# Banded heads as query columns of two 64-key blocks with packed sinks, and where q and k are transposed and evacuated (one core, attention plus expert layers)

## The chip, the cores and the metric

One core of one Trainium2 chip. The metric is device time in microseconds; lower is better. A run is called slow when it took over 1.5% longer than the fastest run of the same kernel, and fast otherwise; only fast runs enter a ratio, but the medians given are over all runs. The runs fell on several chips. Kernels are compared only within the same rounds.

Engines: TensorE (PE), VectorE (DVE), ScalarE (ACT), GpSimd (POOL). PSUM is the memory that the matmuls write into; to evacuate is to copy a result out of it. The clock is the share of TensorE's full clock that was granted, by the trace's record of its changes (the clock record). Times in a trace count from the start of the profiled run.

## The reference

```python
# attention: 4 batches, 8 heads, 768 tokens, head size 64; heads 0, 2, 6 are full, the others banded
keep_full   = i >= j
keep_banded = (i >= j) & ((j < 4) | (i - j < 64))      # 4 sink keys and a window of 64
a = softmax(where(keep, q @ k.T / 8, -1e9)); x = a @ v # x: 3072 tokens x 512
# expert layers: every token goes to the expert of its domain_id (8 experts)
out[t] = relu(x[t] @ w1[e]) @ w2[e]
```

## The kernel before

The heads are worked in 16 pairs, four per batch: (0,2) two full heads (RR), (6,7) one full and one banded (RS), (1,3) and (4,5) two banded (SS). For a pair, TensorE puts a mask into PSUM as a matmul with the identity, adds the scores, ScalarE takes the exponential, and the values are multiplied one pair later. In between TensorE transposes q and k of the next pair. Twenty routing items (token counts, ranks, one-hot rows, the map from slots to tokens) are threaded in, mostly on VectorE; two of them, `ranks` and `rows`, have matmuls that wait for VectorE.

PSUM: three wide tiles (1024 fp32) for scores, and two small banks for transposes, values and the routing matmuls.

```python
def tr(t, ...):                      # q and k each in a small bank, in different steps
    ...
        evac = nc.scalar.copy if n == 0 and nm == "q" else nc.vector.tensor_copy
        evac(out=d[:], in_=cell["ps"][:, 0:NSO].rearrange("d t p -> d p t"))
# ... cut
for n in range(NPAIR + 1):
    hooks(n)                         # loads, casts on GpSimd, stores
    R = len(plans[n % 4])            # score tiles: RR 6, RS 5, SS 3
    if R == 3:
        steps = [T["q"] + A, T["k"] + B_]              # A, B_: values of the pair before, head by head
    else:
        steps = [T["q"] + A, T["k"] + B_[:h], B_[h:]]
    for x, step in enumerate(steps):
        scores(n, range(2 * x, min(2 * x + 2, R)))
        if n >= 1 and route:
            route.pop(0)()           # one routing item after each group of scores
        run(step)
```

The softmax here doesn't subtract the row's maximum and nothing guards it: scores larger than these inputs give would overflow.

## Time and profile before

Median 215.31 us in three runs (212.85 to 215.68). The profile is of a slow run (227.59 us); a profile on another chip (225.17 us) has its attention part within 2 us of it. Read from the two traces by the q transposition in each pair, which is one easily found row per pair:

| | before | before, other chip |
|---|---|---|
| first scores of pair 0 | 8.52 | 8.52 |
| q transposition for pair 10 | 59.14 | 58.41 |
| q transposition for pair 15 | 83.46 | 81.97 |
| first expert-layer matmul | 97.80 | 94.52 |

The timeline of TensorE at the start of pair 1 (columns: start, duration, engine, line, operation, result and operands, sizes, count, and in brackets the idle time before it with what ended it):

```profile
14.78 0.62 PE L306 MATMUL sp<-qT,kT 64*128 64x512 f16 x9
15.33 0.51 PE L286 MATMUL tpq<-c16s,q 128*128 128x128 f16 x6
...
17.36 0.30 PE L484 MATMUL prior_ps<-rs,c16s 128*128 128x8 f16 x3
17.74 0.49 PE L286 MATMUL tpk<-c16s,k 128*128 128x128 f16 x6
```

The rank matmuls (prior_ps) stand between two groups without any wait, and six transposes take 0.5 us.

### The profile page before, as it was taken

How to read it: one execution, taken by the hardware profiler on the slowest of the kernel's cores; microseconds unless marked ns; L12 is line 12 of the kernel's file. 1: busy time of each engine (PE TensorE's matmuls, PEld its weight loads, DVE VectorE, ACT ScalarE, POOL GpSimd, SP SyncE). 2: the span in 40 equal slices, each digit the busy share in tenths (PEclk: the TensorE clock that was granted, in tenths of full speed). 3: DMA queues.
4: the chain of work that ended last, by engine and by line, in shares of the span. 5: the costliest groups of instructions: out<-in, count | busy, mean ns of one | idle time of the engine just before them, and what ended most of it. 6: DMA issues, size and time to landing. Idle time of an engine off the chain costs nothing. (4 is left out here: it accounts for less than half of the span.)

```text
span 225.8 us, 4791 instructions
## 1 busy us (share of the span) xinstructions
PE 187.7 (83%) x1959; PEld 123.0 (54%) x1959; DVE 98.7 (44%) x200; ACT 92.1 (41%) x120; POOL 120.7 (53%) x170
## 2 busy tenths in 40 slices
PE   0888779989899999289969499999999999998430
PEld 0455455656576675169958495455554564443210
DVE  1448999998977574142110105520244002433210
ACT  2487248855775885115634260025400461000000
POOL 2446768774666884740178743657566403027611
PEclk9999999999999999859997999999999999999955
DMA  6999999999999998399649999996999999704321
GB/s 190 325 298 312 288 299 298 328 291 281 280 343 320 216 249 172 107 170 235 167 90 212 207 256 209 256 219 185 183 185 280 214 220 279 201 17 168 131 93 48
DMA packets 42909, 49.79 MB, mean 220 GB/s; under 512 B 27263, under 2 KB 35712, under 8 KB 42882
## 3 DMA queue, kind: packets, MB, share of 16 engines
q0 software_dynamic: 7936, 26.75, 52.9%
q1 hardware_dynamic: 34802, 22.62, 35.2%
q8 instruction: 17, 0.28, 0.5%
q10 hardware_dynamic: 144, 0.07, 0.2%
q14 instruction: 10, 0.08, 0.1%
HBM read 56.76 MB, written 10.49 MB: 298 GB/s over the span
## 5 line engine op out<-in xcount | busy, mean ns | idle before, releaser
L343 ACT ACTIVATE eT<-sp 128x1024 f16<-128x1024 f32 (+2 forms) x68 | 57.4, 919 | 28.5 <-PE sp L306 26.0
L718 ACT ACTIVATE hT<-h 128x512 f16<-128x512 f32 (+2 forms) x48 | 32.1, 668 | 62.5 <-PE h L711 61.3
L711 PE MATMUL h<-xT,w 128*128 128x256 f16 (+2 forms) x384 | 53.6, 302 | 0.4 <-issue 0.4
L727 POOL DMA_INDIRECT out_dram<-oute,out_i x27 | 27.0, 1001 | 38.7 <-DVE oute L725 33.0
L711 PEld LDWEIGHTS <-w 128*128 128x128 f16 x384 | 40.6, 117 | 11.5 <-issue 0.6
L761 PE MATMUL o<-w,hT 128*128 128x512 f16 x184 | 41.9, 379 | 0.0
L725 DVE COPY oute<-o 128x512 f32<-128x512 f32 x23 | 15.9, 691 | 55.2 <-PE o L761 47.6
L663 POOL DMA_INDIRECT xe<-x_tok,map_i x24 | 24.4, 1019 | 23.7 <-SPq L932 13.1
L396 PE MATMUL av<-ve,eT 128*128 128x65 f16 (+1 forms) x472 | 24.6, 196 | 5.5 <-remote 3.0
L761 PEld LDWEIGHTS <-hT 128*128 128x128 f16 x184 | 17.5, 98 | 19.8 <-issue 0.8
L396 PEld LDWEIGHTS <-eT 128*128 128x128 f16 (+1 forms) x572 | 21.6, 101 | 10.9 <-DVE xb L409 3.9
L306 PE MATMUL sp<-qT,kT 64*128 64x192 f16 (+8 forms) x276 | 23.6, 273 | 2.8 <-DVE kT L292 2.6
L306 PE MATMUL sp<-c16s 128*128 128x128 f16 (+1 forms) x132 | 21.6, 271 | 1.9 <-ACT eT L343 1.7
L158 POOL CAST q<-q 128x768 f16<-128x768 f32 x15 | 12.4, 829 | 15.0 <-DMA q<-in_q_dram 6.4
L178 POOL CAST ve<-v 128x384 f16<-128x384 f32 x32 | 17.0, 558 | 5.5 <-DMA v<-in_v_dram 5.5
L696 DVE COPY xT<-xtp 128x1024 f16<-128x1024 f16 (+1 forms) x16 | 8.8, 552 | 24.0 <-PE xtp L683 24.0
L409 DVE TENSOR_TENSOR xb<-av,rcp 128x384 f16<-128x384 f32 x32 | 17.8, 557 | 1.1
L292 DVE COPY qT<-tpq 128x768 f16<-128x768 f16 x15 | 14.3, 953 | 8.9 <-PE tpq L286 8.9
L158 POOL CAST k<-k 128x768 f16<-128x768 f32 x15 | 13.6, 904 | 7.9 <-PE tpk L286 4.3
L306 PEld LDWEIGHTS <-kT 64*128 64x128 f16 (+1 forms) x276 | 10.8, 96 | 12.4 <-DVE kT L292 4.3
L292 DVE COPY kT<-tpk 128x768 f16<-128x768 f16 x16 | 15.2, 953 | 3.7 <-PE tpk L286 3.7
L753 ACT COPY oute_last<-o_last 128x128 f32<-128x128 f32 x2 | 0.5, 265 | 32.2 <-DVE oute_last L753 32.2
(83 smaller groups left out, 148.4 us busy)
## 6 DMA issues: line engine op xcount, KB each, us to landing
w<-in_moe_w_dram POOLq DMA_DIRECT2D x16, 1024.0 KB
q<-in_q_dram SPq DMA_DIRECT2D x16, 384.0 KB, 5.9
k<-in_k_dram SPq DMA_DIRECT2D x16, 384.0 KB, 6.0
v<-in_v_dram SPq DMA_DIRECT2D x32, 192.0 KB, 5.8
x_tok<-xb SPq DMA_DIRECT2D x4, 768.0 KB, 7.9
out_dram<-oute,out_i POOLq DMA_INDIRECT x27
xe<-x_tok,map_i POOLq DMA_INDIRECT x24
c16s<-c SPq DMA_DIRECT2D x1, 336.5 KB, 5.5
```

Of the source, the lines that this page charges most:

```text
L158: eng.tensor_copy(out=t[:].rearrange("p t h d -> p h t d"), in_=q32_t[nm, n][:])
L178: nc.gpsimd.tensor_copy(out=ve_t[b][:, :, h, 0:D], in_=v_t[b, pi][:, hh])
L292: evac(out=d[:], in_=cell["ps"][:, 0:NSO].rearrange("d t p -> d p t"))
L306: nc.tensor.matmul(out=sp[rows, c : c + w], lhsT=lhsT, rhs=rhs, start=bank not in begun, stop=True, skip_group_check=True,)
L343: nc.scalar.activation(out=eT[n, r // 3][:, r % 3, c0:c1], in_=sp[:, c0:c1], func=AF.Exp, scale=scale)
L396: nc.tensor.matmul(out=ps[m0:m1, it, :], lhsT=eT[n, r // 3][:, r % 3, c : c + w], rhs=rhs, start=(x == 0), stop=(x == len(mms) - 1), skip_ ...
L409: nc.vector.tensor_tensor(out=xb[b][:, :, h * D : (h + 1) * D], in0=ps[:, :, 0:D], in1=rcp[:].unsqueeze(2).to_broadcast([P, NSO, D]), op=A ...
L663: nc.gpsimd.indirect_dma_start(out=xe_of(pr, g), out_offset=None, in_=x_d[0 : 1 + nb * S, :], in_offset=bass.IndirectOffsetOnAxis(ap=map_i ...
L711: nc.tensor.matmul(out=pv[:, a, c0:c1], lhsT=w_t[e, 1][:, c // 2, c % 2, fc * 512 + fr : (fc + 1) * 512 : 4], rhs=xT_t[e][:, c, c0:c1], st ...
L718: nc.scalar.activation(out=hT_t[e][:, 2 * f2 : 2 * f2 + 2, c0:c1], in_=pv[:, :, c0:c1], func=AF.Relu)
L727: inst = nc.gpsimd.indirect_dma_start(out=out, out_offset=bass.IndirectOffsetOnAxis(ap=out_i[:, s : s + 1], axis=0), in_=o[:], in_offset=None,
L761: nc.tensor.matmul(out=ps[:], lhsT=hT_t[e][:, f, g * P : (g + 1) * P], rhs=w_t[e, 2][:, f // 4, f % 4, :], start=(f == 0), stop=(f == 7),)
```

## The change

Its intent: a banded head's scores are laid out so that each query column meets only the two 64-key blocks that its window can reach, which removes one of three score tiles; the sinks of several heads are packed into one stationary tile of v; q and k are transposed in one go, in a wide tile for SS pairs (with q evacuated by ScalarE) and in both small banks otherwise; the value matmuls of the half blocks need a shifted copy of v (vm), made by VectorE. Its core:

```diff
+    def copy_vm(n):                                     # two copies per pair with a banded head
+        for rows, t0 in ((slice(0, 64), 1), (slice(64, P), 0)):
+            nc.vector.tensor_copy(out=vm_t[b][rows, ...], in_=ve_t[b][rows, t0 : t0 + NSO - 1, ...])
...
+    def transposes(n, q_evac, wide):
+        if wide:
+            ps = ps_s.tile([P, 2, 8, P], FP16, tag="sp", ...)      # q and k in one wide tile
+        else:                                                      # q and k in the two small banks
+            halves = [ps_b.tile([P, 8, P], FP16, tag="b", ...)[:] for nm in "qk"]
+        ... 12 transposes ...
+        for x, (nm, store, evac) in enumerate((("q", qT, q_evac), ("k", kT, nc.vector.tensor_copy))):
+            evac(out=d[:], in_=halves[x][:, 0:NSO].rearrange("d t p -> d p t"))
...
-            if n >= 1 and route:
-                route.pop(0)()
-            run(step)
+            run(step)
+            if n >= 1 and R > 1 and (R, x) != (3, 1):   # R counts steps now: RR 3, RS 2, SS 1
+                for fn in route[:2]:
+                    fn()
+                del route[:2]
```

```diff
-        if R == 3: steps = [T["q"] + A, T["k"] + B_]
-        else:      steps = [T["q"] + A, T["k"] + B_[:h], B_[h:]]
+        steps = {1: [tr + av0 + av1 + post],            # post: copy_vm(n)
+                 2: [tr + post, av0 + av1],
+                 3: [tr, av0, av1]}[R]
```

Not shown: the new masks and score bins, the value matmuls in 64-row halves, six zero-filled sink tiles at the start with six small loads.

## The prediction

> **What bounds the kernel now.** I read the page first (state, busy shares, slices), then engine windows cut at the first scores of each batch, then the timeline of single pairs, then the waits. The profiled execution is a slow one (227.59 us against a median of 215.31), so I use it for durations and order inside the attention part, where the clock was granted in full, and not for the end-to-end time.
>
> ```profile
> span 225.8 us, 4791 instructions
> PE 187.7 (83%) x1959; PEld 123.0 (54%) x1959; DVE 98.7 (44%) x200; ACT 92.1 (41%) x120; POOL 120.7 (53%) x170
> ...
> PE   0888779989899999289969499999999999998430
> ...
> DVE  1448999998977574142110105520244002433210
> ACT  2487248855775885115634260025400461000000
> ```
>
> The slices (5.6 us each) split the run: about 16 slices of attention, where VectorE is at 8 to 9 in slices 4 to 10 and falls afterwards, a hole at slice 17, then the expert layers, which the change does not touch. The windows say the same in numbers (columns: engine busy us and count, clock, DMA share, GB/s). The four batches of four head pairs are the first four lines; the last two are pairs 1 to 9 and pairs 10 to 15.
>
> ```profile
> 14.78:32.33 17.55, 13.66 (x225) 9.52 (x224) 15.53 (x37) 9.34 (x11) 12.14 (x23) 1.00 1.16 296
> 32.33:52.24 19.91, 18.48 (x293) 12.41 (x294) 19.60 (x39) 14.31 (x17) 16.15 (x25) 1.00 1.09 299
> 52.24:72.48 20.24, 19.11 (x317) 12.99 (x318) 16.10 (x38) 14.42 (x17) 11.21 (x23) 1.00 1.12 311
> 72.48:90.04 17.56, 17.01 (x279) 11.43 (x277) 10.46 (x20) 13.54 (x16) 12.54 (x21) 1.00 1.00 222
> 14.78:64.19 49.41, 43.13 (x694) 29.09 (x693) 45.32 (x101) 32.88 (x39) 34.67 (x60) 1.00 1.12 298
> 64.19:90.04 25.85, 25.13 (x419) 17.26 (x418) 16.36 (x31) 18.74 (x22) 17.38 (x31) 1.00 1.05 256
> ```
>
> Two regimes. In pairs 1 to 9 VectorE is busy 45.3 of 49.4 us (19.60 of 19.91 in the second batch), because the token routing (49 instructions, 21 us, added up from the timeline) is threaded between the evacuations. In pairs 10 to 15 TensorE is busy 25.13 of 25.85 us and VectorE has room. ScalarE binds only in the pair of two full heads: six exponentials, some 5.5 us. One stretch of VectorE's timeline shows how a transpose evacuation, a division and a routing step follow each other without a gap:
>
> ```profile
> 43.68 0.68 DVE L584 TENSOR_TENSOR ohl<-c16s,lof 128x512 f16<-128x512 f16 x1
> 44.28 0.95 DVE L292 COPY qT<-tpq 128x768 f16<-128x768 f16 x1
> 45.15 0.18 DVE L408 RECIPROCAL rcp<-av 128x6 f32<-128x6 f32 x1
> 45.36 0.56 DVE L409 TENSOR_TENSOR xb<-av,rcp 128x384 f16<-128x384 f32 x1
> 45.84 1.07 DVE L584 TENSOR_TENSOR ohl<-c16s,lof 128x512 f16<-128x512 f16 x1
> ```
>
> The DMA queues move about 300 GB/s throughout (share above 1), but TensorE waits for GpSimd's casts only 1 us in all, so loads are near a limit and not yet the limit.
>
> **What the Trainium skill says.** "TensorE: Matmul & The Clock Gate", section "Wait — 56ns, not 53.3ns?": a warm matmul costs N/2.4 GHz plus 2.5 ns, and starts never come closer than about 25 ns. The trace agrees: six transposes take 0.51 us from first start to last end, one lasts 0.22, so (0.51 - 0.22)/5 = 58 ns; 21 value matmuls of 65 columns take 0.80 us, one 0.195, so 30 ns. "TensorEngine Tiling (Array Packing)", section "Tiling Modes": 64x64 gives four independent tiles, and a mode switch drains the array; column tiling disables the fast weight load. Nothing in this trace shows four tiles at once; 64-column weight loads do read longer (111 ns against 98). "VectorE: DVE Perf Modes", section "The perf-mode tier table": a 16-bit copy inside SBUF can go at 4x, one out of PSUM at most at 2x. The PSUM side agrees (768 elements in 953 ns, below even 2x with that strided output); no plain fp16 SBUF copy is in the trace, the nearest is a 672-element multiply in 417 ns. "TensorE: Matmul & The Clock Gate", section "Why this matters for your kernels": an idle gap over about 3 us cools the clock. Here the granted clock fell to 0.64 and 0.50 between 94 and 100 us after such a hole.
>
> **The change part by part.** Write RR for two full heads, RS for one full and one banded, SS for two banded; a batch has one RR, one RS, two SS.
>
> ScalarE. SS drops its third score tile: 8 exponentials of 704 columns, 6.1 us. RS drops from 4x1024+256 to 3x1024+640 columns, about 0.7 us each by 1.02 us per 1024, 2.8 us. It takes over seven q evacuations (the one ScalarE did measured 0.80): +5.6 us. Net -3 us on an engine that is busy 75% at most: worth little directly.
>
> TensorE, SS pair. From the timeline of pair 11 (67.69 to 72.15 us): masks 0.97, 12 score matmuls 0.55, q transposes 0.35, values 0.68, small masks 0.16, 6 more scores 0.50, k transposes 0.56, values 0.69: 4.46 us. After: mask columns 2176 to 1536, so 0.97 x 1536/2048 = 0.73; 34 small score matmuls at 30 ns, 1.02, plus about 0.1 for drains; 12 transposes 0.70; 32 value matmuls, as many as before, 1.3. Sum 3.85: 0.6 less. This assumes the tiles really overlap; without overlap the scores alone would be near 1.9 us and the gain gone. RS: masks somewhat fewer, seven matmuls net more: TensorE about equal at 4.3 us, but five ScalarE tiles become four (4.5 to 3.8 us); pair 13 ran 4.99 us, so perhaps 0.4 to be had. RR unchanged. The whole order has 140 more weight-load and matmul pairs.
>
> VectorE. Removed: seven q evacuations of 0.953, 6.7 us. Added: 24 half-height copies of v, 8 of 330 and 16 of 660 elements; from the 417 ns row I estimate 0.24 and 0.40 us, 8.3 us. Six zero fills of 512 words at the start: the 256-word one took 272 ns, so 0.53 each and about 4 us with the small ones, from 1.1 us until just when q lands (4.87): 0 to 0.3 us of delay. In pairs 1 to 9 alone: -4 x 0.953 + 6 x 0.24 + 8 x 0.40 = +0.8, so about 46 us of VectorE work in a stretch of 49.4. The change does not relieve the engine that binds there. It also bunches the routing: four steps in each RR and RS pair, none in SS, so RR plus RS of the second batch carry about 16 us of VectorE work against 10 us of the others', and SS about 3 us against 4. The first batch could gain 1 to 2 us (its VectorE was idle 2 us), the third can lose as much: the map matmuls stand on TensorE between two score steps and wait for the last one-hot step.
>
> GpSimd. 20 sink copies (5.2 us) and four fills leave, six load issues come (0.78 us each by the weight loads' rows). Even; not on the path.
>
> The sum. Pairs 1 to 9: -1 us, give or take 2. Pairs 10 and 11: -1.2. Pairs 12 to 15: TensorE -1.6, but hidden in part: the third batch's token store was issued at 77.83, its first gather began at 87.31 and the first gathered transpose at 91.48, while TensorE was through with pair 14's values at 90.04. That chain of 13.7 us does not shorten, so I count a third of it, 0.5. Total about -2.7 us: 215.3 - 2.7 = 212.6.
>
> **The rivals.** (a) VectorE stays the bound in the routing part and the bunching costs more than the slack: the second batch's 98.5% speaks for it, the hole in the first batch against. Pairs 1 to 9 would be 2 us longer and the whole even: 215. (b) The small tiles do not overlap, or each drain costs: SS keeps its 4.46 us; 214 to 216. Longer 64-column weight loads speak for it; the alternating 64-row matmuls (12 in 0.62 us) against. (c) Everything fits: SS at 3.85 us, the copies at their fastest, ScalarE's earlier q evacuations keep TensorE fed, and the store lands sooner in an undisturbed run than in this slow one: 8 x 0.6 + 4 x 0.4 + 1.5 = 8 us, 207. That so many placements were chosen by hand speaks for it. (d) The wait for the gathers grows past 3 us and cools the clock: plus 1 to 3 us.
>
> **Range and chances.** I predict 212.6 us. The range 208.0 to 217.0 holds (a), (b) and most of (c). Faster by over 2% means below 211.0, which needs most of (c): 0.34. Slower by over 2% (above 219.6) needs (a), (b) and (d) together: 0.07. Within 2%: 0.59.
>
> **What would show it.** In the changed profile: an SS pair without routing takes about 3.9 us from scores to scores; VectorE above 90% busy over pairs 1 to 9, which take 47 to 50 us; value copies of 0.24 and 0.40 us; the routed RR and RS pairs each over 6 us; TensorE waiting longer than before ahead of the gathered transposes; expert layers unchanged. Wrong if SS pairs stay at 4.4 us (tiles do not overlap), if pairs 1 to 9 fall well below 47 us (then the evacuations' order, not VectorE's sum, had set the pace), or if the time moves in the expert layers.

## The result, and the profile after

232.75 us median in four runs (229.62 to 233.26), against 215.5 us for the kernel before in the same call. The ratio of the fast runs is 1.0796, 95% interval 1.0612 to 1.0981. (A ratio is the mean time of one kernel's fast runs over that of the other's of the same rounds, so it is not quite the ratio of the medians.) The change is slower. Run again on another chip (below, with the experiments), it was 1.0833.

The profiled run (233.26 us) counts as slow, 1.6% above the fastest. The repeat was profiled in a fast run, and its pairs 1, 4, 9 and 13 (12.95, 6.77, 10.92 and 5.45 us) bear out what is read here.

The page of the changed kernel; the second line is TensorE's busy share in tenths per slice, the third the granted clock in tenths, which answers to the page shown in the prediction:

```profile
span 231.5 us, 5105 instructions
...
PE   0675985997775985994995789999999999999960
...
PEclk9985599599999599998599999999999999999996
```

The clock has fives inside the attention part (slices 4, 5, 8, 14, counted from 1). In the kernel before it had none there. Windows of single pairs, cut at their first scores (pairs 1, 4, 9 and 14), and the whole of pairs 1 to 9; the clock is the third number from the end:

```profile
16.19:28.97 12.78, 9.95 (x91) 6.06 (x91) 5.38 (x14) 3.66 (x4) 6.01 (x10) 0.50 1.13 282
38.90:46.48 7.58, 6.97 (x73) 4.02 (x74) 6.62 (x21) 5.17 (x6) 2.56 (x4) 0.57 1.07 296
68.17:79.50 11.33, 8.84 (x112) 5.73 (x113) 7.50 (x19) 3.66 (x4) 2.50 (x4) 0.76 1.04 308
100.43:104.75 4.32, 3.50 (x88) 2.63 (x88) 1.50 (x3) 2.63 (x3) 0.00 (x0) 1.00 0.73 229
16.19:79.50 63.31, 49.50 (x771) 32.58 (x772) 46.70 (x107) 31.86 (x36) 29.51 (x48) 0.80 1.05 277
```

Pairs 1 to 9 took 63.31 us where the kernel before took 49.41 (its window is in the prediction). VectorE is busy 46.70 us of them, almost what it was (45.32): it was not given much more to do, it was waited for. The pair lengths, scores to scores:

| pair | kind | before | after |
|---|---|---|---|
| 1 | RS | 5.21 | 12.78 |
| 2 | SS | 6.85 | 4.49 |
| 4 | RR | 5.60 | 7.58 |
| 9 | RS | 5.60 | 11.33 |
| 12 | RR | 5.60 | 6.61 |
| 13 | RS | 4.84 | 5.45 |

Values of pair 14 were done at 107.25 us, not 90.04, and the first expert-layer matmul came at 112.38 instead of 97.80. From there to the end of the span it took 119.1 us in this trace and 119.0 in the repeat. All of the loss is in the attention part.

The waits of the changed kernel (who waited for whom, us in total, times, longest):

```profile
DVE kT L315 <- ACT qT L315: 10.7, 6, 2.8
...
PE sp L342 <- DVE kT L315: 6.9, 8, 1.5
...
PE av L392 <- DVE vm L186: 3.0, 3, 2.3
PE prior_ps L484 <- DVE rs L473: 2.8, 1, 2.8
```

And TensorE's timeline in pair 1, to be laid beside the rows of the kernel before:

```profile
15.90 0.36 PE L325 MATMUL sp<-c16s 128*128 128x128 f16 x2 [0.48 <-ACT eT L353]
16.19 2.58 PE L342 MATMUL sp<-qT,kT 64*128 64x512 f16 x20
18.70 0.82 PE L306 MATMUL tpq<-c16s,q 128*128 128x128 f16 x6
...
22.99 0.31 PE L484 MATMUL prior_ps<-rs,c16s 128*128 128x8 f16 x3 [2.83 <-DVE rs L473]
...
25.27 2.49 PE L392 MATMUL av<-ve,eT 128*128 128x65 f16 x42
```

Two things are to be seen. TensorE stood still for 2.83 us in front of the rank matmuls. And everything around them runs at half speed, already before that halt: six transposes take 0.82 us, not 0.51; the 20 score matmuls take 2.58 us, while the same 20 take 1.69 in pair 13; the 42 value matmuls take 2.49, in pair 5 1.44. Adding up these differences over pair 1 gives 4.15 us (0.89 scores, 0.65 transposes, 0.22 masks, 0.68 scores, 1.05 values, 0.66 masks). 2.83 + 4.15 = 6.98 of the 7.57 us that pair 1 is longer. In pair 9 the halts are 0.71 and 1.77 us (ahead of the map matmuls), the slow matmuls behind them 0.68 + 1.05 + 0.66 = 2.39: 4.9 of 5.7 us.

```profile
71.34 0.68 PE L595 MATMUL map_ps<-ohh,ohl 128*128 128x56 f16 x20 [0.71 <-DVE qT L315]
73.80 0.28 PE L595 MATMUL map_ps<-ohh,ohl 128*128 128x56 f16 x4 [1.77 <-DVE ohl L584]
```

Why pair 1 is slow from its first matmul is seen in pair 0. The same 3.41 us of it, in the kernel before and in the changed one (windows; TensorE's busy time is the second number after the window, the clock the third from the end):

```profile
12.65:16.06 3.41, 2.74 (x40) 1.72 (x39) 1.69 (x4) 2.82 (x4) 1.43 (x2) 1.00 1.19 300
12.65:16.06 3.41, 1.98 (x18) 0.81 (x14) 0.73 (x1) 3.06 (x4) 1.69 (x3) 1.00 1.29 265
```

The kernel before stopped for 0.19 and 0.48 us in it and ran on at full clock; the changed kernel stopped for 0.68, 0.26 and 0.48 us, waiting for exponentials, and its clock fell at 16.06.

Pairs 2 to 4 show two more things, in one stretch of the timelines of ScalarE, VectorE and TensorE:

```profile
31.61 0.81 ACT L315 COPY qT<-tp 128x768 f16<-128x768 f16 x1
32.45 0.96 DVE L315 COPY kT<-tp 128x768 f16<-128x768 f16 x1 [1.84 <-ACT qT L315]
33.46 0.87 PE L342 MATMUL sp<-qT,kT 64*128 64x128 f16 x34 [0.72 <-DVE kT L315]
34.71 3.13 DVE L186 COPY vm<-ve 64x660 f16<-64x660 f16 x2
37.90 0.19 PE L392 MATMUL av<-vm,eT 128*64 128x65 f16 x1 [2.28 <-DVE vm L186]
```

In the banded pairs k is evacuated only when ScalarE is through with q, which itself stands behind two exponentials: VectorE idles 1.84 us, then TensorE 0.72. And two copies of v took 3.13 us, though the median of all 24 is 0.38 us and the shortest 0.24; GpSimd was casting during all of it. TensorE waited 2.28 us, and pair 4 then ran at a clock of 0.57.

From this come four theories. A: the routing, bunched behind the steps, halts TensorE at `ranks` and `rows`. B: the order q before k in the shared tile delays every banded pair. C: the small score tiles and their interleaving cost TensorE itself. D: the v copies on VectorE are slow beside GpSimd and delay what stands behind them. Over all of them stands the clock: is the half speed a cause of its own, set off by any of these halts, or only a companion?

### The profile page after: what moved, and what is told of

It reads as the page before. It is cut to its first block, busy times and chain, and to the rows that moved or that the text cites. A ratio compares the mean times of both kernels' runs of the same rounds, so it can differ in the third digit from the quotient of the medians.

```text
span 231.5 us, 5105 instructions
## 1 busy us (share of the span) xinstructions
PE 188.0 (81%) x2099; PEld 123.2 (53%) x2099; DVE 104.3 (45%) x229; ACT 90.3 (39%) x115; POOL 116.6 (50%) x152
## 5 line engine op out<-in xcount | busy, mean ns | idle before, releaser
L353 ACT ACTIVATE eT<-sp 128x1024 f16<-128x1024 f32 (+2 forms) x56 | 50.7, 953 | 43.1 <-PE sp L342 42.8
L711 PE MATMUL h<-xT,w 128*128 128x256 f16 (+2 forms) x384 | 51.7, 295 | 0.4 <-DVE xT L690 0.4
L711 PEld LDWEIGHTS <-w 128*128 128x128 f16 x384 | 39.3, 115 | 11.2 <-DVE xT L690 0.6
L725 DVE COPY oute<-o 128x512 f32<-128x512 f32 x23 | 15.9, 692 | 51.7 <-PE o L761 49.5
L342 PE MATMUL sp<-qT,kT 64*64 64x128 f16 (+6 forms) x436 | 28.2, 272 | 6.9 <-DVE kT L315 6.9
L761 PEld LDWEIGHTS <-hT 128*128 128x128 f16 x184 | 17.5, 98 | 19.8 <-issue 0.8
L392 PE MATMUL av<-ve,eT 128*128 128x65 f16 (+1 forms) x372 | 21.1, 209 | 3.5 <-DVE qT L315 1.5
L342 PEld LDWEIGHTS <-kT 64*64 64x64 f16 (+2 forms) x436 | 12.6, 109 | 19.6 <-DVE kT L315 8.7
L325 PE MATMUL sp<-c16s 128*128 128x128 f16 (+2 forms) x112 | 18.9, 294 | 1.9 <-ACT eT L353 1.9
L186 DVE COPY vm<-ve 64x660 f16<-64x660 f16 (+1 forms) x24 | 13.9, 577 | 0.2
L683 PE MATMUL xtp<-c16s,xe 128*128 128x128 f16 x96 | 8.6, 227 | 5.4 <-DMA xe<-x_tok,map_i 5.4
L315 DVE COPY qT<-tpq 128x768 f16<-128x768 f16 x8 | 7.7, 958 | 11.4 <-PE tpq L306 11.3
```

The costliest lines, as they stand in the source:

```text
L325: nc.tensor.matmul(out=sp[:, c : c + w], lhsT=id_sb, rhs=c16[:, col : col + w], start=c // 512 not in begun, stop=True, skip_group_check=True,
L342: nc.tensor.matmul(out=sp[o : o + m, c : c + w], lhsT=kT[n][rows, k0 : k0 + m], rhs=qT[n][rows, i0 : i0 + w], start=False, stop=True, skip ...
L353: nc.scalar.activation(out=eT[n, r // 3][:, r % 3, c0:c1], in_=sp[:, c0:c1], func=AF.Exp, scale=scale)
L392: nc.tensor.matmul(out=ps[m0 : m0 + m, it, :], lhsT=eT[n, r // 3][rows, r % 3, c : c + m], rhs=rhs[:, 0 : D + 1], start=(cell["n"] == 1), ...
L711: nc.tensor.matmul(out=pv[:, a, c0:c1], lhsT=w_t[e, 1][:, c // 2, c % 2, fc * 512 + fr : (fc + 1) * 512 : 4], rhs=xT_t[e][:, c, c0:c1], st ...
L761: nc.tensor.matmul(out=ps[:], lhsT=hT_t[e][:, f, g * P : (g + 1) * P], rhs=w_t[e, 2][:, f // 4, f % 4, :], start=(f == 0), stop=(f == 7),)
```

## The experiments

Sixteen runs besides the first result, all correct. "Place of q(15)" is the start of the q transposition for pair 15, a measure of the attention part: 82.0 and 83.5 in the two traces before, 101.2 in the first trace of the changed kernel, 99.7 in its repeat. Each trace is one execution; those of the routing spread, k first, no interleaving and, in the fourth call, the routing left out are of slow runs.

### First call: each theory alone

The changed kernel was not in this call, so the ratios here cannot be set beside its 1.08; the places can.

The kernel before once more, for a trace on this chip.

> The kernel before, for a profile in an undisturbed execution (the one at hand is slow, 227.6 us). All theories: about 214 us, the attention part (scores of pair 0 to values of pair 14) as long as in the slow profile, 81.5 us; what the slow execution had too much lies after it.

225.17 us; 224.32 median. As expected in the attention part; this is the second column of the table above.

**Routing spread.** One routing item after each group of scores, as in the kernel before.

```diff
-            run(step)
-            if n >= 1 and R > 1 and (R, x) != (3, 1): ... two items
+            if n >= 1 and route:
+                route.pop(0)()
+            run(step)
```

> Changed kernel with the token routing handed out as in the kernel before: one step after each scores group in every pair, instead of two at a time in pairs with a full head. Theory A (TensorE stands before the routing matmuls until VectorE delivers, and its clock then falls to half): pairs 1 and 9 fall from 12.8 and 11.3 us to about 6 each, pair 4 from 7.6 to about 6.3, and the whole from 232.8 to about 220. Theory B (in banded pairs the k evacuation waits behind ScalarE's exponentials and q copy, so everything on VectorE comes late): at most 2 us gained. Theory C (the small score tiles and v copies cost TensorE and VectorE more than the change saves): nothing gained, 231 to 233.

242.47 us (three slow runs, one fast at 234.53, so no ratio). The expected gain did not come. Pair 9 shrank as theory A said, and the rank matmuls no longer waited, but pair 1 still ran at half speed, from about 17 to 27.3 us, and new halts with new falls of the clock appeared in other pairs (4 and 12 among them). Place of q(15): 100.6. So in this trace, of a slow run, the loss is there without the bunching; the one fast run has no trace.

**k first.** The two evacuations swapped everywhere.

```diff
-        for x, (nm, store, evac) in enumerate((("q", ...), ("k", ...))):
+        for x, (nm, store, evac) in list(enumerate((("q", ...), ("k", ...))))[::-1]:
```

> Changed kernel with k evacuated before q in every pair, so that VectorE's copy no longer waits for ScalarE's. Theory B: banded pairs without routing fall from 4.32 to about 3.7 us, the pair of two full heads from 6.6 to about 5.7, the wait of VectorE's k copy for ScalarE's q copy (10.7 us) is gone, and the whole is 6 to 8 us shorter, about 226. Theory A: pairs 1 and 9 stay at 11 to 13 us, the whole gains 3 us at most. Theory C: banded pairs stay above 4.2 us.

234.63 us, ratio 1.0349 (1.0221 to 1.0477). Banded pairs went from 4.3 to 3.3 us where VectorE had room (q transposition to q transposition), place of q(15) 95.3. Pairs 1 and 9 stayed long. B is real and partial.

**No interleaving.** In RS pairs first all scores of the full head, then all of the banded.

> Changed kernel with the score matmuls of the full-plus-banded pair in two blocks (all of the full head, then all of the banded one) instead of alternating. Theory C in the form that alternating tile shapes costs TensorE time: the 20-matmul group falls from 1.69 to about 1.2 us, the pair without routing from 5.45 to about 4.9, four pairs together some 2 us. Theories A and B: within 1 us of the changed kernel, 232.

239.63 us, ratio 1.0647 (1.0532 to 1.0762), place of q(15) 98.0. RS pair 13 fell from 5.45 to 5.21 us only. C is small; the 34 small score matmuls take 0.87 us in every warm pair of every trace, close to what was predicted for them.

### Second call: the clock by itself, the copies, and all together

**The changed kernel again**, on the chip of this call.

> The changed kernel again, unaltered, so that this call has it on the same chip as its variants. Every theory expects what the first measurement gave, about 1.08 times the kernel before; by a spread between chips anything from 1.05 to 1.09. Pair 1 about 12.5 us, pair 4 about 7.5, pair 9 about 11.5.

232.64 us, ratio 1.0833 (1.0725 to 1.0941).

**v copies on GpSimd**, right behind the cast of v.

```diff
-            nc.vector.tensor_copy(out=vm_t[b][rows, ...], ...)
+            nc.gpsimd.tensor_copy(out=vm_t[b][rows, ...], ...)     # called from cast_v
```

> The changed kernel with the copies of v (two per pair with a banded head) issued on GpSimd right behind its cast of v, and none on VectorE. If those copies are a main cost (theory D: 13.9 us of VectorE, slow where GpSimd works at the same time, one of them holding TensorE for 2.28 us in pair 3 and so cooling it for pair 4), the wait of the value matmuls for vm goes, pair 4 falls from 7.6 to about 5.6 us, and the routing of pairs 5 to 9 comes earlier: 4 to 8 us off the changed kernel. If the cost sits in where the routing matmuls stand (theory A) and in the q and k order (theory B), only 2 to 3 us go, and pairs 1 and 9 stay within 1.5 us of 12.8 and 11.3.

228.05 us, ratio 1.0614 (1.0515 to 1.0713), 4.6 us less. The wait for vm is gone and pair 3's 2.28 us with it; the interval that holds pair 4 fell only from 7.6 to 7.35 us, less than expected. Place of q(15) 94.8. On the mechanism: the Trainium skill, "SBUF — State Buffer", section "Who interferes with whom", says that VectorE copies in a fast two-port mode and GpSimd lock each other out for a whole instruction. The traces agree: the copies vary from 0.24 to 2.78 us on VectorE beside GpSimd's work. The run does not separate this lock from the time that the copies take in any case.

**Fillers.** Matmuls nobody reads, put where TensorE stood still; no wait is taken away, 138 matmuls are added.

```diff
+    def fill(ps, k, start=True):
+        for i in range(k):
+            nc.tensor.matmul(out=ps, lhsT=id_sb, rhs=id_sb[:, 0 : ps.shape[-1]], start=start, stop=True, ...)
# 10 and 12 in pair 0 between score groups, 44 before the rank matmuls, 44 before the first vm matmul, 28 before the last map matmuls
```

> The changed kernel with idle TensorE time filled: 128x128 matmuls whose result nobody reads, 22 in pair 0, 44 ahead of the rank matmuls in pair 1, 44 ahead of the first value matmul that waits for vm in pair 3, 28 ahead of the last four map matmuls in pair 9. No wait is taken away, and TensorE has more to do. If the cold clock is what makes pairs 1, 4 and 9 long (by the trace 4.2, 2.0 and 2.8 us: 20 score matmuls in 2.58 us against 1.69, 42 value matmuls in 2.49 against 1.44), these come back: pair 1 about 9, pair 4 about 5.6, pair 9 about 8.5 us, and the total 7 to 9 us below the changed kernel. If the clock is only a sign of something else (a limit on power or on the memory), the same matmuls stay at 2.4 to 2.6 us and the total does not fall or rises by 1 to 4 us.

226.09 us, ratio 1.0554 (1.045 to 1.0657): 6.5 us less than the changed kernel, with more work. TensorE's timeline in pair 1:

```profile
17.08 1.69 PE L352 MATMUL sp<-qT,kT 64*128 64x512 f16 x20
...
20.25 2.62 PE L298 MATMUL prior_ps<-c16s 128*128 128x128 f16 x44 [0.71 <-DVE qT L325]
22.86 0.29 PE L497 MATMUL prior_ps<-rs,c16s 128*128 128x8 f16 x3
...
24.21 1.44 PE L404 MATMUL av<-ve,eT 128*128 128x65 f16 x42
```

The rank matmuls start at 22.86, as late as before (22.99): VectorE's result was awaited just as long. But 20 scores take 1.69 again and 42 values 1.44. The half speed is a cause of its own. Place of q(15) 93.6. The effect of the fillers in pair 0 shows in more than this trace: in all eight traces with the 22 fillers of pair 0 the 20 scores of pair 1 take 1.69 us, in all seven traces of the changed order without them 2.12 to 2.58. In the eight, by the clock record, TensorE comes to full speed at 12.5 to 15.8 us and still has it in those scores; in the seven it lost it again at 16.1 to 17.1 us or came to it only at 25.5 to 28.8. In the trace of this run the clock is 1.00 from 15.8 to 101.1 us, where the repeat of the changed kernel has 27.3 us of half speed before 99.7. So the clock cost some 6 us of the 17; the rest, by difference, is left to the halts and waits themselves. This is the one experiment that separates the clock from the halts, and it came out a little under what was expected (7 to 9 us).

**All together**: k first, routing spread, v copies on GpSimd, and the 22 fillers in pair 0.

> All that the theories name at once on top of the changed kernel: k before q everywhere, one routing step after each group of scores (as in the kernel before), copies of v on GpSimd, and the 22 filler matmuls in pair 0. If theories A, B and D together are the whole loss, pairs 1 and 9 come to about 6 us, banded pairs to 3.5 us, and the total is at or below the kernel before: ratio 0.97 to 1.00. If something else in the change costs (small tiles, the expert part's later start), the ratio stays above 1.02.

215.97 us, ratio 0.999 (0.9874 to 1.0106): the whole loss is back, 16.7 us. Place of q(15) 82.2. Cut into windows of 4 us, the granted clock is 1.00 in each up to 88 us (until 15.7 us that is only the absence of a record: the first ten fillers still take 1.25 us, the next twelve 0.84). In pair 1 the values wait 0.57 us and run at full speed; after the attention part TensorE stands still for 6 us until the first gathered rows come:

```profile
21.46 1.43 PE L403 MATMUL av<-ve,eT 128*128 128x65 f16 x42 [0.57 <-DVE qT L326]
...
92.77 1.31 PE L694 MATMUL xtp<-c16s,xe 128*128 128x128 f16 x8 [6.09 <-DMA xe<-x_tok,map_i]
```

### Third call: what is left, and the reverse test

**RR split**: in the combination, q and k of the pair after a full one transposed in different steps again, values head by head.

> The combination that came out level with the kernel before (k first, routing after each group of scores, v copies on GpSimd, 22 fillers in pair 0) with one more thing undone: in the pair of two full heads q and k of the next pair are transposed in different steps, and the values go head by head, as in the kernel before. In that combination the step from one q transposition to the next takes 7.3, 6.6 and 7.4 us from pairs 4, 8 and 12, against 5.5 to 5.7 before, with TensorE waiting 0.72 and 0.52 us for the evacuations. If holding both small banks at once for the transposes is the cause, these come to 5.6 to 6.0 and TensorE ends its last values 4 us earlier, at about 83 us; the total falls by 0 to 2 us only, because the first gathered rows come when GpSimd gets to its gathers (89.2 us). If VectorE's sum is the cause, they stay above 6.5.

225.38 us against 225.64, ratio 0.9839 (0.976 to 0.9917). The intervals stayed at 7.1, 6.8 and 7.1 us: the case that was expected did not come, and its premise was wrong too ("above 6.5" came true, but not for the reason given there). These intervals end behind the first scores of the RS pair, which are 20 matmuls (1.69 us) in the changed kernel and 9 (0.62) in the kernel before; 1.07 us of the supposed loss was the ruler. This chip gave the kernel before 225.6, so the ratio cannot be laid beside the 0.999 of the other.

**Gathers earlier**: in the combination, the late v copies and the zero fills of the gathered-row tiles on VectorE.

> The same combination, but from pair 13 on the v copies stand on VectorE and the four zero fills of the gathered-row tiles stand on VectorE as well, so that GpSimd reaches its first gather earlier. In the combination GpSimd ended its last v copy at 85.3 us, its fills at 89.0, issued the first gather at 89.17, and TensorE stood still for 6.1 us. If the gathers' issue is what the end of attention waits for, the first gather goes out at 84 to 86 us, the wait falls to 2 to 4 us, and the total falls by 2 to 4 us. If the store of the third batch is what they wait for, nothing moves.

223.95 us, ratio 0.9905 (0.9816 to 0.9993). The first gather went out at 82.88 us, not 89.17, and yet the first gathered transposes stand at 92.29 (92.77 in the combination) and the first expert-layer matmul at 94.77 (95.36 in the combination). Issuing sooner moved the rows hardly at all; the 2 to 4 us did not come.

**Both.**

> Both of these together. If both causes are right, the ratio to the kernel before is 0.96 to 0.98; if the gathers then wait for the stores, 0.98 to 0.995.

223.16 us, ratio 0.9829 (0.9752 to 0.9906): 1.7% under the kernel before from two fast runs, with the interval clear of 1 but the difference under 2%.

**The reverse**: the kernel before, with only the bunched routing put in.

```diff
-            if n >= 1 and route:
-                route.pop(0)()
             run(step)
+            if n >= 1 and R > 3 and (R, x) not in ((6, 1), (5, 2)):
+                ... two items
```

> The kernel before with one thing of the change put in: the routing stands behind the work of a step, two items at a time, four in each pair with a full head, none in pairs of banded heads. Heads, tiles, transposes and copies are those of before. If the bunching and the halts of TensorE that it makes (with the cold clock behind them) are the main cause, it costs 5 to 12 us: a wait for rs ahead of the rank matmuls in pair 1 and for the one-hot rows in pair 9, each over 1 us, with matmuls at half speed behind at least one of them. If the bunching hurts only together with the change's other parts (the longer k order, the v copies), it costs 0 to 3 us and the clock stays up.

228.72 us, ratio 1.0144 (1.0081 to 1.0208): about 3 us, between the two expectations, with the halt and the half speed of the first (in pair 9 the wait for the one-hot rows was 0.62 us, not over 1):

```profile
17.93 0.30 PE L484 MATMUL prior_ps<-rs,c16s 128*128 128x8 f16 x3 [1.84 <-DVE rs L473]
...
18.47 1.46 PE L306 MATMUL sp<-qT,kT 64*128 64x512 f16 x6
```

Six score matmuls took 0.82 us at that place before. But some SS pairs, free of routing now, became shorter by 1 to 2 us and paid part of it back: the intervals of pairs 2 and 3 are 4.85 and 3.82 us against 6.85 and 5.49.

### Fourth call: one edit left out of the combination at a time

> The combination without the filler matmuls. The last q transposition stood at 82.2 us with all four edits. If TensorE's stops in pair 0 (0.36 to 0.68 us each, where it waits for exponentials) are what leaves it cold at the start of pair 1, pair 1 runs at half speed again and the last q transposition comes at 84.5 to 87; time against the kernel before 1.00 to 1.02. If the halts for routing were what cooled it, the fillers do nothing and it stays within 0.5 of 82.2.

> The combination with the routing left in the changed kernel's places (two at a time behind a step of the pairs with a full head). The bunching put into the kernel before cost 3 to 4.5 us of attention time. If it costs the same here, the last q transposition comes at 85 to 87; if it is the main cause, and worse with small tiles, at 88 or later. Ratio to the kernel before 1.00 to 1.03.

> The combination with the v copies back on VectorE. They are 13.9 us of VectorE in the changed kernel and gave back 4.6 us alone. In the combination VectorE is the bound in pairs 1 to 9, so the copies should lengthen those: last q transposition at 85 to 89. If they can hide now that k comes first, under 84. The zero fills on GpSimd may hold late copies up, as they held a routing step of 28 elements for 3.4 us in the run with the routing spread.

> The combination with q evacuated before k again. The banded pairs took 4.3 us in the changed kernel and 3.3 to 3.5 in all runs with k first, and there are eight: 6 to 8 us, last q transposition at 87 to 90, ratio to the kernel before 1.01 to 1.03. If other waits fill the place, under 85.

All on one chip. The kernel before had a median of 225.71 us there, but four of its seven runs were slow; the three fast ones took 220.35 to 223.51. The combination itself ran on another chip; a near relative of it (gathers earlier) on a chip of the same slower kind had its q(15) at 81.75, so that place may be compared:

| left out | median us | fast runs, us | ratio | place of q(15) | over 82.2 |
|---|---|---|---|---|---|
| fillers in pair 0 | 228.19 | 227.21 to 229.12 | 1.0268 (1.0129 to 1.0407) | 88.3 | 6.1 |
| routing spread | 234.12 | 232.20 to 234.32 | 1.051 (1.0363 to 1.0658) | 92.1 | 9.9 |
| v copies on GpSimd | 234.27 | 230.16, 233.12 | none (spread of the runs) | 94.3 | 12.2 |
| k first | 232.04 | 227.05, 229.90 | none (spread of the runs) | 87.0 | 4.8 |

The fillers and the v copies cost more than expected, the routing fell in the worse of its two cases, k first came out at its lower edge. The sum, 33 us, is nearly twice what all four together cost (17.5 = 99.7 - 82.2). The costs do not add up: most of the single slips set off the same thing. Between 16 us and the place of q(15) the clock record has no half speed in the combination; it has 10.2 us of it without the fillers, 17.1 without the routing spread, 17.1 without the v copies moved, but 3.4 without k first (there TensorE mostly stood still, 2.79 us of it before the values of pair 4). Without the fillers pair 1 was 2.1 us longer (q transposition to q transposition), nearly all of it at half speed by its rows (20 scores 2.58 us) though the clock still reads 1.00, the pairs behind it fell in with GpSimd's and VectorE's work in another way, and in pair 4 the values had to wait until k was evacuated (which fits the small bank that held it). The timeline of TensorE, and windows of 1 us (the clock is third from the end):

```profile
37.02 0.19 PE L393 MATMUL av<-ve,eT 128*128 128x65 f16 x1 [1.58 <-DVE kT L316]
...
40.30 2.58 PE L343 MATMUL sp<-qT,kT 64*128 64x512 f16 x20
```

```profile
40.00:41.00 1.00, 1.00 (x9) 0.27 (x9) 0.97 (x4) 0.11 (x1) 0.42 (x1) 0.50 1.19 253
...
48.00:49.00 1.00, 1.00 (x14) 0.71 (x12) 0.60 (x3) 0.00 (x0) 1.00 (x2) 0.50 1.11 355
```

The clock fell to 0.50 at about 39.1 us and came back at about 49.4 (from the means of the windows at both ends), although TensorE is busy in all of every window between. Without the v copies moved, the same happened twice; the second time a routing step of 28 elements on VectorE held everything behind it up for 4 us while GpSimd filled tiles with zeros (timelines of VectorE and of GpSimd):

```profile
81.04 4.00 DVE L635 TENSOR_SCALAR mb<-mu 128x28 int32<-128x28 int32 x1
```

```profile
81.36 3.63 POOL L838 MEMSET xe<- 128x1024 f16 x4
```

The same step takes 0.16 to 0.63 us in the other traces looked at, and 3.38 with the routing spread.

## Why the prediction was wrong, by its own steps

**"Pairs 1 to 9: -1 us, give or take 2"** is the step that failed. Measured: +13.9 us (49.41 to 63.31). The working took VectorE's sum as the bound and found it nearly unchanged (45.3 to about 46; measured 46.7, so the sum was right). What it left out is the order: the kernel before had placed each VectorE result before TensorE wanted it, and the change put `ranks`, the map rows, k behind q, and the v copies in front of matmuls that need them at once. The prediction saw the bunching ("the map matmuls stand on TensorE between two score steps and wait for the last one-hot step") and sized it at 1 to 2 us from the slack of VectorE. It was 2.5 us of halts in pair 9 and 2.8 in pair 1.

**Rival (d), the cooled clock, 1 to 3 us**, was the right mechanism in the wrong place. The prediction looked for it in the hole before the expert layers. It came in pairs 1, 4 and 9 (in pair 1 set off in pair 0), and filling the halts gave back 6.5 us of the 17 with every wait left in. The prediction's reading of the Trainium skill ("TensorE: Matmul & The Clock Gate", section "Why this matters for your kernels": an idle gap over about 3 us cools the clock) was too coarse: in pair 0 three stops of 0.68, 0.26 and 0.48 us, from 13.4 to 15.9 us, were followed by half speed at 16.1. The prediction's own trace spoke against its reading: the hole before the expert layers lasts from 93.66 to 96.71 us, but the clock fell at about 94.6, less than 1 us into it, after stops of 1.44 and 0.69 us. (Its clause on the fast weight load stands on the tiling page under "Restrictions", not "Tiling Modes".)

**"TensorE, SS pair: 3.85 us"**: the work was about as sized or less (3.50 us busy in pair 14, small scores 0.87 for 1.02 predicted; the tiles do overlap), the pair took 4.32 us because k waited for q. With k first it takes 3.3 to 3.5 us. Rival (b) therefore fell.

**"RS about equal, 0.4 to be had"**: 5.45 us where the kernel before took 4.84 (scores to scores; the prediction's 4.99 is in no view on record); the 20 scores of its first step take 1.69 us where 9 took 0.62, of which the order of full and banded heads explains 0.25. **"RR unchanged"**: 6.61, not 5.60 us (pair 12); with k first alone 5.55.

**v copies "0.24 and 0.40 us, 8.3 us"**: the shortest are as estimated, the sum was 13.9 us, since some last up to 2.78 us beside GpSimd's work. **The start, "0 to 0.3 us"**: 1.2 us, since q's cast came at 5.77 instead of 4.87 us behind the zero fills and k's evacuation stood behind q's.

**What was right**: the expert part shows no change by the traces, VectorE's busy time in pairs 1 to 9 is nearly the predicted one (though 74% of the longer stretch, not above 90%), ScalarE's saving was worth little.

What stays open: how much each cause holds "by itself" has no answer, since leaving out any one of the four edits costs 5 to 12 us and the four together 17.5. Why the clock stays low so much longer in some places (about 10 us without a stop in the run without fillers) is only half settled: by the clock records of all eighteen traces, every stretch of half speed in the first 125 us lasts 3.41, 6.83, 10.24 or 13.65 us, which is one to four times 3.41. A halt can so cost several such steps, but what decides after each step is not shown. Nor is what holds back the gathered rows after attention.

## What to carry to other kernels

When a tuned schedule is rearranged, compare not only each engine's busy sum but, for each matmul that waits for another engine, whether its input is ready earlier or later than before; a sum that stays the same says nothing about it. A halt of TensorE can cost more than itself: in pair 9 halts of 2.48 us were followed by 2.39 us lost at half speed, and in pair 0 three short stops close together, 1.42 us in all, were enough. Test for it by filling the halts with matmuls nobody reads. And undo one thing at a time out of a version that works, not only out of the one that fails: by the place of q(15) in the traces the single repairs here gave back between nothing and 6.1 us, and together 17.5.

## What the Trainium skill lacked or had wrong

- "TensorE: Matmul & The Clock Gate": its figure of idle gaps over about 3 us is too generous here. Half speed followed stops of 0.68, 0.26 and 0.48 us between 13.4 and 15.9 us (pair 0), and stops of 1.58 and 0.52 us (run without the fillers). The page's section "A second HAM failure mode: psum-queue depth-cycling" does speak of micro-idles that make the clock oscillate, but gives no size for them.
- The same page has one or more busy windows of about 3.4 us for the clock to come back, and does not say when it takes more than one. Here it stayed at 0.50 for about 10 us with TensorE busy throughout (run without the fillers, 39.1 to 49.4 us), and for over 13 us, with a halt of 2.83 us in it, in pair 1 of the changed kernel (the record has 10.24 and 13.65 us, three and four times 3.41).
- Its warning that the clock in a trace is not fully to be trusted holds, and the page lacks one form of it: before the first change on record the reading is 1.00 whatever the clock. In every trace six transposes take 0.82 us at the start at a reading of 1.00; without interleaving the first 20 scores of pair 1 take 2.28 us at 1.00 (1.44 in pair 13), and with k first 2.58 us (1.69). Durations of equal rows are the safer sign.
- "SBUF — State Buffer": its lock between VectorE and GpSimd agrees with the traces. It has no example of how little work can be caught: a 28-element integer operation took 4.00 us beside a series of zero fills, 0.18 us in the changed kernel.
- No page has an example of a transposed k or q, left in a small PSUM bank, holding back the value matmuls of the pair before. A wait of 1.58 us in the run without the fillers fits it, but no run isolates it.
